# Seed exponents of a Fourier-domain SSM kernel: one product and four exponentials per chunk instead of 25 exponentials, with a new instruction order

## The chip, the cores and the metric

The kernel runs on one core of one Trainium2 chip. The metric is the device time of one execution in microseconds (us). Besides the times there is one profiled execution, whose instructions are recorded on the engines: PE (matrix multiplications, with PEld for its weight loads), DVE (VectorE), ACT (ScalarE), POOL (GpSimd), and SP, whose queue issues nearly all DMA transfers.

## The reference, cut to what matters

Two state-space layers A and B (L = 2048 positions, D = 512 channels, N = 128 states) see the same input u, and a gate mixes their results:

```python
dt = jnp.exp(log_dt)[:, None]
logdA = dt * (A_re + 1j * A_im)
P = jnp.exp(logdA[:, :, None] * l[None, None, :])      # l = 0 .. 2047
K = jnp.einsum("dn,dnl,dn->dl", Cc, P, dt * Bc).real
y = irfft(rfft(pad(u)) * rfft(pad(K)))[:L] + u * Dskip
...
out = g * a + (1 - g) * b          # g = sigmoid((u * gate_w).sum(-1))
```

The magnitude of the powers P is exp(al · l), with al = dt · A_re (one number for each state and channel). Powers of all l are products of a few seeds: l is split into digits, and exp(al · l) is the product of one factor per digit.

## The kernel before, in words

**Tiling.** The channels are cut into NCH = 8 chunks of 64 channels; with the two layers a chunk has CH = 128 columns. The 128 states lie on the partitions. A chunk is built in NG = 8 groups of G = 16 columns, so there are NT = 64 tables T = 0 .. 63.

**Seeds.** `seed(c, parts)` writes for a chunk the factors exp(al · l) into two tiles. `ml` (128 x 128 x 16) has in columns 0 to 7 the factors for l = 0 to 7, in columns 8 to 15 those for l = 0, 8, .. 56. `mh` (128 x 128 x 12) has in columns 0 to 7 those for 256 l, in columns 8 to 11 those for 64 l, l = 0 to 3. Each has two copies, used in turn by even and odd chunks. Before the change every column is one ACTIVATE of 128 elements (one number per channel column, so the writes are 16 or 12 floats apart), with the factor l in its scale; columns that are all ones are set once by `memset`. 25 such ACTIVATEs per chunk are recorded as five steps of five (line 523). The input is row 0 of the tile `par`, which for chunks 1 to 7 is loaded from DRAM (`prd`) by `load_par`; `par` has two buffers. `seed_angles` then makes the integer phases `sa` on POOL and multiplies columns 8 to 11 of `mh` by the amplitude rho, also on POOL.

**Tables.** For each T, `tables` makes phases `ang` on POOL (two additions or products, line 271), magnitudes `mr` from `ml` and `mh` (two products, line 271, mostly POOL), sine `s`, sine of the half `ang` and its square `sq` on ACT (three ACTIVATEs, line 284), and then on DVE `ei` = s · mr and `mr` = (sq − 1) · mr (lines 271 and 281, four instructions). `mr` has three buffers, `ang` and `ei` two, `s` and `sq` one each, in PSUM. In every third table the product of `ml` is made on DVE from a copy of eight columns in PSUM (`c`, copied by ACT). PE then multiplies these tables (`kgen`, line 588), a copy takes the result to `kt`, and `first` (line 605) begins the transform.

**The convolution.** Per chunk: `spectrum` (line 618) on PE, the product with the stored spectrum of u on DVE (`y`, line 690), the inverse `back` (line 710), copies to `z`, a store to DRAM `zb`, a transposed load to `f`, and `fin` (line 742) with a copy to `o` and the output's store. `u_spectra` and `gated` run once near the start. Copies out of PSUM (`copy`) may be made by ACT (line 294) or by DVE (line 296); `tt` with "any" by POOL or by DVE.

**What sets the order.** All work is first listed as steps, with their dependences. The string `ORDER` then gives the order in which the steps are issued; a number with `b` takes the second engine of the step's choice (DVE instead of ACT for a copy, DVE instead of POOL for an "any" product). Each engine works through its own steps strictly in this order, and SP issues its transfers in it. A buffer of a ring goes to the next user in this order.

**Tables of functions.** Exp and Sin lie in different function tables of ACT, so a change between them puts an ACT_TABLE_LOAD ahead of the instruction. Sine takes the table numbered 9 in the code, exponentials table 0.

Of the kernel before, what the change touches and what calls it, by code (L numbers as in the profile page):

```python
# [45 lines left out]
def constants():  # L46
# [7 lines left out]
    for q in range(4):  # L54
# [17 lines left out]
                                   np.full((128, 1), math.pi / 4)], 1).astype(f32)  # L72
# [10 lines left out]
6 7 11 8 9 4 2 182 3 1 82 83 0 84 475 86 186 183 18 19 20 24 21 22 23 25 26 27 28 29 30 31 32 33 34 35 37 88 184b 185b 38 17  # L83
36 85 190 326 40 44 45 39 41 42 46 47 48 366 76 49 50 51 59 79 73 71 75 187 52 53 188 189 54 55 56 57 138 58 191 193b 61 62
67 63 60 68 192 64 69 91 14 351 87 13 218 194 15 16 98 65 70 92 93 101 94 95 89 96 43 72 66 353 77 354 78 90 74 100 99 195
102 357 104 103 105 219 113 197b 196b 198 200 355 356 221b 114 360 358 359 199 201 385 203 205 386 361 107 204 206 106 220
226 127 222 327 202 207 210 213 208 209 211 212 129 80 97 12 368 369 383 367 81 10 384 362 108 363 109 110 111 215 214 370
364 216 365 223 112 116 115 371 224 373 122 121 117 123 374 225 372 388 124 118 119 120 387 375 227 217 1403 230 125 126 128
131 134 376 228 389 136 133 231 352 132 137 135 130 5 1406 229 429 232 377 233b 244 390 378 245 391 392 393 249 394 251 395
430 250b 397 398 399 400 401 246 402 403 479 247 477 476 480 478 141 396b 404 405 406 142 143 239 144 252b 145 146 248 1414  # L90
253 148 149 234 150 151 152 407 254 240 431 416 414 427 415 154 139 140b 153 235b 155 236 418 408 379 419 420 409 237 483 417
421 422 428 410 445 446 447 147 448 241 242 156 157 432 380 381 423 159 424 435 158 436 411 433 434 437 413b 438 382 412 160
458 459 481 255 262 175 238 258 484 449 450 257 256 425 439 161 163 452 451 426 440 485 460 482 441 461 162 259 165 166 260
261 453 172 171 173 174 454 263 462 463 265b 167 164 455 168 169 612 611 464 264 609 613 177 266 179 243 176 328 330 331 290
329b 465 267 269b 268b 466 456 457 610 487 467 468 280 282 281b 469 283b 488 470b 294 284 486 170 180 499 501 616 489 502 490
491 492 471 500 442 493 518 519 516 517 494 472 444 443 503 504 495 496 506 332 275 505 473 474 531 333 507 508 520 521 509
276b 497 510 498b 522 511 532 523 524 529 533 530 277 285 278 287 270 272 286 534 535 288 525 526 536 547 549 550 548 512 537
538 334 335 608 279 289 527 336 551 539 540 552 271 553 560 562 561 554 555 528b 541 337 273 564 542 513 563 556 339 178 338
557 558 579 514 515 567 568 580 565 559 566 581 577 543 578 582 593 591 592 594 1407 1408 569 570 585 1404 544 586 583 546
584 545 340 587 588 1405 595 596 341 571 572b 598 342 1415 1426 614 618 615 573 619 599 1416 597 1425 617 181 1417 1409 1410  # L100
1411 274 1412 589 633 590 622 623 349 345 1427 600 1418 1419 601 574 602 575 576 624 603 620 621 649 347 343 625 634 626 1420
# [100 lines left out]
def ssm_mix(ctx: ExitStack, tc: tile.TileContext, a, out, dry=False):  # L202
# [123 lines left out]
    def memset(name, o, *keys):  # L326
        op("pool", "memset", 128, lambda _: pool.memset(o(), 1.0), (), keys or [(name,)])
# [184 lines left out]
    def seed(c, parts):  # L512
# [3 lines left out]
        for k0, kn in parts:  # L516
            ks = slice(k0, k0 + kn)
            for n in range(0, len(cols), 5):
                some = cols[n:n + 5]

                def exps(_, ks=ks, some=some):
                    for tile, j, l in some:
                        act.activation(out=t(*tile)[:, ks, j], in_=t("par", c)[:, 0, ks].bitcast(F32), func=AF.Exp, scale=float(l))  # L523
# [311 lines left out]
```

## Time and profile before

| | |
|---|---|
| median of 3 runs | 477.8 us (475.12 to 482.99) |
| the profiled execution's own time | 472.5 us |
| its span, first to last instruction | 470.7 us |
| mean granted clock of TensorE | 0.971 |
| busy: PE / DVE / ACT / POOL | 394.9 / 416.0 / 386.2 / 338.8 us |
| ACT_TABLE_LOADs | 31, 1.283 us each |
| ACTIVATEs of `seed` | 200 |

The span is the recorded part; 1.8 us lie around it. Busy time is time in which at least one instruction of the engine runs. Of consecutive instructions on an engine the end of one overlaps the start of the next, so the mean duration times the count can exceed the busy time: a recorded ACTIVATE of `seed` lasts 423 ns, but five in a row take 1.3 us.

### The profile page before, as it was taken

How to read it: one execution, taken by the hardware profiler on the slowest of the kernel's cores; microseconds unless marked ns; L12 is line 12 of the kernel's file. 1: busy time of each engine (PE TensorE's matmuls, PEld its weight loads, DVE VectorE, ACT ScalarE, POOL GpSimd, SP SyncE). 2: the span in 40 equal slices, each digit the busy share in tenths (PEclk: the TensorE clock that was granted, in tenths of full speed). 3: DMA queues.
4: the chain of work that ended last, by engine and by line, in shares of the span. 5: the costliest groups of instructions: out<-in, count | busy, mean ns of one | idle time of the engine just before them, and what ended most of it. 6: DMA issues, size and time to landing. Idle time of an engine off the chain costs nothing.

```text
span 470.7 us, 21838 instructions
## 1 busy us (share of the span) xinstructions
PE 394.9 (84%) x9616; PEld 356.4 (76%) x9616; DVE 416.0 (88%) x518; ACT 386.2 (82%) x676; POOL 338.8 (72%) x317
## 2 busy tenths in 40 slices
PE   4797786799968879998898988879598888999935
PEld 3786685689857768787798977778587877898934
DVE  6999889999999999999899999998789999996610
ACT  3889979999988999998899999998789898791110
POOL 2593859599977989796999689878929899650010
PEclk9899899999998999999999999999999999999987
DMA  7866852836555565876465646764838667567793
GB/s 220 276 198 205 246 161 78 249 120 224 183 157 157 133 160 180 212 206 178 132 180 153 206 132 190 193 182 117 195 105 218 167 192 213 152 184 187 212 244 89
DMA packets 74542, 84.53 MB, mean 180 GB/s; under 512 B 5456, under 2 KB 60112, under 8 KB 73392
## 3 DMA queue, kind: packets, MB, share of 16 engines
q1 hardware_dynamic: 74304, 82.75, 62.0%
q8 instruction: 75, 1.23, 1.1%
q0 software_dynamic: 144, 0.39, 0.3%
q14 instruction: 19, 0.16, 0.1%
HBM read 51.48 MB, written 31.65 MB: 177 GB/s over the span
## 4 chain that ended last, share of the span: by engine, by line
PE 35%; DVE 25%; ACT 21%; issue 11%; DMA 4%; SPq 3%; DVEq 0%; POOL 0%; ACTq 0%
PE c L618 8%; PE c L605 8%; DVE mr L281 6%; PE c L588 6%; PE c L742 5%; PE c L710 4%; DVE y L690 4%; ACT s L284 4%; DVE ei L271 4%; ACT ang L284 3%; ACT sq L284 3%; SPq L289 3%; ACT ml L523 2%; DVE ei L281 2%; PE c L439 2%
## 5 line engine op out<-in xcount | busy, mean ns | idle before, releaser
L281 DVE SCALAR_TENSOR_TENSOR mr<-sq,mr 128x1024 f32<-128x1024 f32 (+1 forms) x128 | 117.4, 947 | 1.9 <-ACT sq L284 1.5
L271 POOL TENSOR_TENSOR mr<-ml 128x1024 f32<-128x1024 f32 x43 | 84.3, 1960 | 12.3 <-PE c L588 7.7
L271 POOL TENSOR_TENSOR ang<-par,cint 128x512 int32<-128x512 int32 x64 | 67.5, 1055 | 31.0 <-ACT sq L284 15.9
L271 DVE TENSOR_TENSOR ei<-s,mr 128x1024 f32<-128x1024 f32 x64 | 77.7, 1214 | 4.1 <-ACT s L284 2.8
L588 PE MATMUL c<-mr 128*32 128x64 f32 x2048 | 64.7, 223 | 14.8 <-DVE mr L281 7.3
L605 PE MATMUL c<-small,kt 128*64 128x128 f32 x1024 | 66.3, 283 | 10.9 <-issue 5.0
L690 DVE TENSOR_TENSOR y<-c,u 128x1024 f32<-128x1024 f32 x57 | 68.7, 1214 | 4.3 <-PE c L618 1.7
L284 ACT ACTIVATE s<-ang 128x1024 f32<-128x1024 int32 x64 | 65.9, 1029 | 6.5 <-POOL ang L271 4.5
L605 PEld LDWEIGHTS c<-small,kt 128*64 128x64 f32 x1024 | 58.2, 141 | 15.4 <-issue 6.3
L271 POOL TENSOR_TENSOR mr<-mh 128x512 f32<-128x512 f32 x63 | 67.7, 1080 | 2.4 <-PE c L588 2.4
L271 POOL TENSOR_TENSOR ang<-sa 128x512 int32<-128x512 int32 x64 | 68.6, 1073 | 0.2
L284 ACT ACTIVATE ang<-ang 128x1024 f32<-128x1024 int32 x64 | 67.7, 1058 | 1.2
L284 ACT ACTIVATE sq<-ang 128x1024 f32<-128x1024 f32 x64 | 66.0, 1032 | 3.2 <-DVE mr L281 2.3
L588 PEld LDWEIGHTS c<-mr 128*32 128x32 f32 x2048 | 48.6, 110 | 25.5 <-issue 9.9
L588 PE MATMUL c<-ei 128*32 128x64 f32 x2048 | 64.1, 221 | 3.2 <-issue 3.2
L710 PE MATMUL c<-y,vv 64*64 64x128 f32 x1792 | 59.9, 274 | 4.6 <-issue 2.7
L710 PEld LDWEIGHTS c<-y,vv 64*64 64x64 f32 x1792 | 50.9, 134 | 10.6 <-issue 5.2
L618 PE MATMUL c<-xa,w 128*128 128x128 f32 x384 | 52.8, 287 | 3.5 <-DVE vv L414 1.3
L618 PE MATMUL c<-xb,w 128*128 128x128 f32 x384 | 50.0, 282 | 4.7 <-DVE xb L296 1.3
L588 PEld LDWEIGHTS c<-ei 128*32 128x32 f32 x2048 | 50.6, 111 | 3.6 <-issue 3.6
L618 PEld LDWEIGHTS c<-xa,w 128*128 128x128 f32 x384 | 46.4, 194 | 7.7 <-issue 3.6
L618 PEld LDWEIGHTS c<-xb,w 128*128 128x128 f32 x384 | 45.1, 191 | 8.5 <-issue 3.1
(109 smaller groups left out, 661.9 us busy)
## 6 DMA issues: line engine op xcount, KB each, us to landing
zb<-z SPq DMA_DIRECT2D x31, 512.0 KB, 3.9
u<-us SPq DMA_DIRECT2D x57, 256.0 KB, 4.4
f<-zb SPq DMA_DIRECT2D x28, 512.0 KB, 5.2
us<-z SPq DMA_DIRECT2D x16, 512.0 KB, 3.7
uin<-in_uk_dram SPq DMA_DIRECT2D x16, 256.0 KB, 3.9
f<-in_ut_dram SPq DMA_DIRECT2D x8, 512.0 KB, 5.3
out_dram<-o SPq DMA_DIRECT2D x29, 128.0 KB, 3.2
par<-prd SPq DMA_DIRECT2D x7, 320.0 KB, 3.9
```

What stands on the lines that cost most here:

```text
L271: lambda e: (dve if e == "dve" else pool).tensor_tensor(out=out(), in0=in0(), in1=in1(), op=o),
L281: lambda _: dve.scalar_tensor_tensor(out=out(), in0=in0(), scalar=s, in1=in1(), op0=o0, op1=o1), reads, writes, port=port)
L284: op("act", "act", n, lambda _: act.activation(out=out(), in_=in_(), func=func, **{k: v() if callable(v) else v for k, v in kw.items()}), ...
L289: lambda e: (sp if e == "sp" else pool).dma_start(out=out(), in_=in_()), reads, writes, touch=touch)
L439: pe.matmul(t(*ps)[:, CH * i:CH * i + CH], V(x)()[:, CH * i:CH * i + CH], dgv()[:, k, i], start=True, stop=True)
L523: act.activation(out=t(*tile)[:, ks, j], in_=t("par", c)[:, 0, ks].bitcast(F32), func=AF.Exp, scale=float(l))
L588: pe.matmul(ps[32 * j:32 * j + 32, o], x[:, 4 * o + j, 64:96], x[:, 4 * o + j, 0:64], start=part == 0, stop=part == 1, tile_position=(0, 3 ...
L605: pe.matmul(t(*ps[g // 4])[64 * r:64 * r + 64, 128 * (g % 4):128 * (g % 4) + 128], t(*x)[:, g], t("small")[:, 128 * r:128 * r + 128], star ...
L618: pe.matmul(view()[:, :, k], t("w2", j // 2)[:, 4 * (j % 2) + k], t(*x1)[:, 4 * j + k], start=True, stop=True)
L690: op("dve", "tt1", 1024, lambda _: dve.tensor_tensor(out=t(*y).rearrange("p h s f d -> p h s (f d)"), in0=fv().rearrange("p s f d -> p s ( ...
L710: pe.matmul(bank_of(x)[64 * e:64 * e + 64, CH * q:CH * q + CH], v[:, 0:64] if h else v[:, 32:96], t(*ys[f // 4])[64 * x:64 * x + 64, h, :, ...
L742: pe.matmul(t(*ps)[64 * r:64 * r + 64, DC * i:DC * i + DC], t("gsi")[:, 4 * k + i, s, 64 * r:64 * r + 64], t(*f)[:, 8 * k + 2 * i + r, DC ...
```

## The change

`seed` now first writes, for the whole chunk, the eight products al · l for l = 0 to 7 into columns 0 to 7 of `ml` (one instruction of 1024 elements; the factors 0 to 7 lie in eight new columns of the constant `small`). Four ACTIVATEs follow, each with input from those columns: `mh` columns 0 to 7 with scale 256 (1024 elements), `mh` columns 8 to 11 with scale 64 (512), `ml` columns 8 to 15 with scale 8 (1024), and `ml` columns 0 to 7 in place (1024). The columns for l = 0 come out of the exponential too, so the six memsets of `ml` and `mh` are gone.

```diff
-        cols = [(mh, l, 256 * l) for l in range(1, 8)] + [(mh, 8 + l, 64 * l) for l in range(4)]
-        cols += [(ml, l, l) for l in range(1, 8)] + [(ml, 8 + l, 8 * l) for l in range(1, 8)]
+        runs = ((mh, 0, 8, 256.0), (mh, 8, 4, 64.0), (ml, 8, 8, 8.0), (ml, 0, 8, 1.0))
         for k0, kn in parts:
             ks = slice(k0, k0 + kn)
-            for n in range(0, len(cols), 5):
-                some = cols[n:n + 5]
-
-                def exps(_, ks=ks, some=some):
-                    for tile, j, l in some:
-                        act.activation(out=t(*tile)[:, ks, j], in_=t("par", c)[:, 0, ks].bitcast(F32), func=AF.Exp, scale=float(l))
...
+            tt("any", kn * 8, lambda ks=ks: t(*ml)[:, ks, 0:8],
+               lambda ks=ks, kn=kn: t("par", c)[:, 0, ks].bitcast(F32).unsqueeze(2).to_broadcast([128, kn, 8]),
+               lambda kn=kn: t("small")[:, 513:521].unsqueeze(1).to_broadcast([128, kn, 8]), OP.mult,
+               par(c, "al") + [("small",)], lq)
+            for tile, j, n, scale in runs:
+                actv(kn * n, lambda tile=tile, j=j, n=n, ks=ks: t(*tile)[:, ks, j:j + n], lambda n=n, ks=ks: t(*ml)[:, ks, 0:n],
+                     AF.Exp, lq, hq if tile == mh else lq, table=0, scale=scale)
...
-    for k in range(2):
-        for n, j in (("mh", 0), ("ml", 0), ("ml", 8)):
-            memset(n, lambda n=n, j=j, k=k: t(n, k)[:, :, j], *((n, k, q) for q in range(CH // QK)))
```

The string `ORDER` is replaced as a whole: every engine's queue stands in another order, and some steps take another engine. Counted over the built programs, per engine: the 200 ACTIVATEs of `seed` become 24 of 1024 elements and 8 of 512; the table loads go from 31 to 21; the eight new products stand on POOL. Of the copies, DVE's `kt` go from 17 to 13, `o` from 6 to 5, `xa` from 12 to 9, `xb` from 15 to 14, `z` from 28 to 19, and ACT's go up by as many (one `o`, four `kt`, four `xa` and `xb`, nine `z`). Of the products `mr` from `ml` in SBUF DVE takes 3 (before none, POOL 43, now 40), of those from `mh` 3 (before 1, POOL 63, now 61). One output store moves from POOL's queue to SP's. PE's work is the same, instruction for instruction, in another order.

ACT, where the seeds of chunk 1 are made (tables of chunk 0 around them; `par_724` and `par_699` are chunk 1's parameters, `ml_1`, `mh_1` its seeds; buffer numbers differ between the programs). Before:

```order
L284 ACTIVATE sq_847<-ang_833 128x1024
L523 ACT_TABLE_LOAD
L523 ACTIVATE ml_1_192<-par_724 128x128 x5
L294 ACTIVATE z_779<-c_841 128x512
L523 ACTIVATE mh_1_194<-par_724 128x128 x10
L523 ACTIVATE ml_1_192<-par_724 128x128 x5
```

Now:

```order
L284 ACTIVATE sq_818<-ang_764 128x1024
L294 ACTIVATE z_767<-c_809 128x512
L284 ACT_TABLE_LOAD
L284 ACTIVATE mh_1_194<-ml_1_192 128x128x8
L284 ACTIVATE mh_1_194<-ml_1_192 128x128x4
L294 ACTIVATE vv_0_199<-c_852 128x512
L284 ACTIVATE ml_1_192<-ml_1_192 128x128x8 x2
L284 ACT_TABLE_LOAD
```

What read `par` on ACT now reads `ml`, which POOL has written just before.

POOL, where the seeds of chunk 4 begin while the tables of chunk 3 start (`par_1053` is chunk 2, `par_1917` chunk 3, `par_2691` chunk 4; chunk 4 takes chunk 2's buffer of `par`). The new program:

```order
L271 TENSOR_TENSOR ang_2569<-par_1053,cint_201 128x16x32
L271 TENSOR_TENSOR ang_2569<-sa_1898 128x16x32
L271 TENSOR_TENSOR mr_2681<-mh_0_193 128x16x32
L271 TENSOR_TENSOR sa_2689<-par_1917,cint_201 128x1536
L271 TENSOR_TENSOR ml_0_191<-par_2691,small_183 128x128x8
L271 TENSOR_TENSOR mr_2694<-ml_1_192 128x16x64
```

Before, POOL had at the same place (`par_1102` is chunk 2, `par_1945` chunk 3) no instruction of chunk 4:

```order
L271 TENSOR_TENSOR ang_2782<-par_1102,cint_201 128x16x32
L271 TENSOR_TENSOR mr_2764<-mh_0_193 128x16x32
L271 TENSOR_TENSOR ang_2782<-sa_1931 128x16x32
L271 TENSOR_TENSOR sa_2786<-par_1945,cint_201 128x1536
L271 TENSOR_TENSOR ang_2788<-par_1945,cint_201 128x16x32
```

The product for chunk 4 stands four places behind the last reader of the buffer into which its input is loaded, and ahead of the first table product of chunk 3.

DVE, at the first tables of chunk 1 (`mr_1297` and `mr_1301` are their magnitudes). Now:

```order
L271 TENSOR_TENSOR mr_1297<-c_1291,ml_1_192 128x16x64
L296 COPY z_1299<-c_1281 128x512
L271 TENSOR_TENSOR mr_1301<-ml_1_192 128x16x64
L296 COPY kt_1295<-c_1303 128x256
L271 TENSOR_TENSOR mr_1297<-mh_1_194 128x16x32
L271 TENSOR_TENSOR ei_1350<-s_1341,mr_1297 128x16x64
```

Before, with the same table of chunk 1 (`mr_1404`):

```order
L296 COPY z_1368<-c_1358 128x512
L296 COPY z_1368<-c_1363 128x512
L271 TENSOR_TENSOR mr_1404<-c_1354,ml_1_192 128x16x64
L296 COPY kt_1347<-c_1370 128x256
L271 TENSOR_TENSOR ei_1445<-s_1420,mr_1404 128x16x64
```

Two products of `ml` and `mh`, which POOL made before, are DVE's here, and one copy of `z` is no longer DVE's.

More of the change, by code (lines that the diff above doesn't have):

```diff
@@ L87 @@
[L87 to L94, printed above, removed]
```

105 lines of the change are left out of this document (51 added, 54 removed), and 32 rows, old and new, of the table ORDER.

## The prediction

> **What bounds the kernel now.** I read the profile from the whole to the part: the page's busy times, a table of stretches, the chain of work that ended last, and the groups by shape.
>
> ```profile
> span 470.7 us, 21838 instructions
> PE 394.9 (84%) x9616; PEld 356.4 (76%) x9616; DVE 416.0 (88%) x518; ACT 386.2 (82%) x676; POOL 338.8 (72%) x317
> core 0: us, PE busy (x) PEld busy (x) DVE busy (x) ACT busy (x) POOL busy (x), PEclk, DMA share, GB/s
> 0.00:20.00 20.00, 10.85 (x115) 9.83 (x116) 15.32 (x46) 12.01 (x29) 5.91 (x14) 0.96 0.83 254
> 20.00:60.00 40.00, 32.98 (x497) 30.62 (x497) 34.50 (x49) 35.08 (x77) 28.78 (x30) 0.93 0.68 211
> 60.00:320.00 260.00, 227.76 (x5636) 204.36 (x5637) 254.01 (x299) 242.60 (x413) 219.87 (x197) 0.99 0.60 170
> 320.00:360.00 40.00, 32.71 (x924) 29.24 (x922) 32.99 (x38) 34.62 (x65) 29.30 (x26) 0.96 0.65 163
> 360.00:425.00 65.00, 58.69 (x1716) 52.57 (x1708) 62.38 (x71) 55.21 (x83) 52.99 (x49) 1.00 0.65 182
> 425.00:471.00 46.00, 31.91 (x752) 29.82 (x752) 16.77 (x19) 6.65 (x14) 2.00 (x4) 0.89 0.70 184
> ```
>
> The 88% of DVE is an average over three parts that differ. From 60 to 320 us DVE is busy for 254.0 of 260 us, 98%; ACT has 242.6 (93%), PE 88%, POOL 85%. In the last 46 us DVE has little to do. The last table's magnitudes end on DVE at 424.9:
>
> ```profile
> 423.05 1.81 DVE L281 SCALAR_TENSOR_TENSOR mr<-sq,mr 128x1024 f32<-128x1024 f32 x2
> ```
>
> What follows (the last products y, the last inverse, store, load, `fin`) is 46 us in which the change does nothing: the same instructions stand behind the last table on PE, and DVE has one copy of `xb` less there. So the time is the moment of the last table plus 46 us, and what counts is how fast DVE gets through the tables. Nevertheless the chain of work that ended last runs often over ACT, as this part of it shows (140 to 200 us, shares of 60 us):
>
> ```profile
> by line: ACT s L284 10.0%; issue 9.8%; ACT ml L523 9.7%; ACT ang L284 8.9%; ACT sq L284 7.8%; PE c L588 7.4%; ACT L523 6.4%; ACT L284 6.4%; DVE y L690 5.8%; DVE mr L281 5.6%; ACT xa L294 4.2%; ACT mh L523 4.1%; PE c L710 3.3%; DVE mr L271 2
> ```
>
> The seeds (ml and mh, L523) are 13.8% of these 60 us, and the table loads (the nameless ACT L523 and L284) 12.8%. But in the same stretches DVE idles for almost nothing: a chain over ACT is not free time on DVE. These two readings are the two forecasts between which I choose.
>
> **ACT, step by step.**
>
> ```profile
> L523 ACT ACTIVATE ml<-par 128x128 f32<-128x128 f32 x112 | 29.5, 423 | 0.1
> L523 ACT ACTIVATE mh<-par 128x128 f32<-128x128 f32 x88 | 24.4, 435 | 0.1
> L523 ACT ACT_TABLE_LOAD x13 | 16.7, 1283 | 0.2
> L284 ACT ACT_TABLE_LOAD x18 | 23.1, 1283 | 1.0 <-PEq L824 0.7
> L284 ACT ACTIVATE ang<-ang 128x1024 f32<-128x1024 int32 x64 | 67.7, 1058 | 1.2
> L294 ACT ACTIVATE z<-c 128x512 f32<-128x512 f32 x63 | 36.0, 596 | 12.0 <-PE c L710 9.3 <-PE c L618 2.7
> L284 ACT ACTIVATE c<-ml 128x128 f32<-128x128 f32 x21 | 5.9, 281 | 0.1
> L294 ACT ACTIVATE kt<-c 128x256 f32<-128x256 f32 x47 | 18.0, 382 | 5.5 <-PE c L588 5.5
> ```
>
> Removed: 29.5 + 24.4 = 53.9 us of seeds, and ten table loads of 1.283, 12.8 us. Added: 24 exponentials of 1024 elements. No row has their form, with runs of eight floats 16 apart in and out. Nearest is `ang`, 1.058 us, in place in SBUF; and `c` from `ml` reads just such runs at 281 ns for 128 elements, no more than a dense copy's slope gives (382 at 256, 596 at 512). The far end is the old form's rate, 53.9/200 = 0.27 us for 128 elements, 2.16 for 1024; the near end is 1.03 (`sq`). I take 1.058, since `c` shows that runs of eight cost nothing to read. With 8 of 512 at 0.6 this makes 25.4 + 4.8 = 30.2 us. Copies taken over from DVE: nine `z` and four `xa`, `xb` at 0.596, four `kt` and one `o` at 0.38, 9.6 us. ACT changes by −53.9 − 12.8 + 30.2 + 9.6 = **−26.9 us**; at the far end of the price it would be +3.5.
>
> **DVE.**
>
> ```profile
> L296 DVE COPY z<-c 128x512 f32<-128x512 f32 x25 | 16.3, 679 | 0.3 <-PE c L710 0.3
> L296 DVE COPY kt<-c 128x256 f32<-128x256 f32 x17 | 7.0, 414 | 2.4 <-PE c L588 2.4
> L271 DVE TENSOR_TENSOR mr<-c,ml 128x1024 f32<-128x1024 f32 x21 | 25.5, 1214 | 1.5 <-ACT c L284 1.5
> L271 DVE TENSOR_TENSOR mr<-mh 128x512 f32<-128x512 f32 x1 | 0.8, 769 | 0.0
> ```
>
> Thirteen copies of 512 go (0.68 each), four `kt` and an `o` (0.41): −10.9 us. Two `mr` from `mh` come (0.77 each). Three `mr` from `ml` with both inputs in SBUF come; this form has no row, between 1.21 (one input in PSUM) and POOL's 1.96. I take 1.3, as the `mh` form shows 0.77 against 0.68 for other work of its size: +3.9. Together **−5.5 us** (−3.5 at the far end).
>
> **POOL.**
>
> ```profile
> L271 POOL TENSOR_TENSOR mr<-ml 128x1024 f32<-128x1024 f32 x43 | 84.3, 1960 | 12.3 <-PE c L588 7.7 <-ACT ml L523 1.7 <-issue 1.1
> L271 POOL TENSOR_TENSOR mr<-mh 128x512 f32<-128x512 f32 x63 | 67.7, 1080 | 2.4 <-PE c L588 2.4
> POOL ang L271 <- ACT sq L284: 15.9, 11, 4.3
> ```
>
> Eight products of 1024 elements at 1.96 are +15.7; three and two tables' products leave, −5.9 and −2.2; the memsets and an output's issue are −2.4. POOL gains 5.2 us. It is hidden: POOL is 85% busy in the middle, and it waits 15.9 us because ACT has not yet freed `ang`; it runs ahead. Without that lead the whole product would come into the path of every chunk (rival three).
>
> **What of it reaches the end.** DVE's 5.5 us lie in the part where it is saturated, so I count them in full. ACT's 26.9 us count only where DVE waited for ACT:
>
> ```profile
> DVE ei L271 <- ACT s L284: 2.8, 4, 1.8
> DVE mr L281 <- ACT sq L284: 1.5, 5, 0.6
> DVE mr L271 <- ACT c L284: 1.5, 2, 1.0
> ```
>
> That is 5.8 us. In a new order some such waits arise elsewhere; I take half, −2.9, with 0 and −5.8 as ends. The start is costed at nothing: four exponentials take the place of two groups of five before the first sine, some 0.6 us earlier, but the chain there lies on PE and DMA. Three more things are left as they are. The wait of 4 us inside a run of PE's multiplications, put down to issue, which idles DVE for 5.1,
>
> ```profile
> 339.79 3.16 PE L605 MATMUL c<-small,kt 128*64 128x128 f32 x28 [4.02 <-issue]
> DVE xb L296 <- PE c L605: 5.1, 1, 5.1
> ```
>
> has no cause in the order that I can see; gone, it is worth up to −5. PE keeps all its instructions and the part behind the last table. The output store that leaves POOL lies in the tail, where POOL waits.
>
> **The sum:** 470.7 − 5.5 − 2.9 = 462.3 us of span, with the 1.8 around it 464.1, against this execution's own 472.5. The median of the runs shown, 477.8, is 1.011 times that execution, so the forecast is 464.1 · 1.011 = **469 us**, 1.8% less. About 2% (below 468.2 or above 487.4) is what a measurement of this kernel can tell from no change, as its runs lie between 475 and 483; the forecast is just inside.
>
> **Rivals.**
>
> *One: the chain over ACT pays in full.* Another part of the chain, 260 to 320 us, looks like the one above:
>
> ```profile
> by line: issue 16.3%; DVE mr L281 11.9%; ACT s L284 8.1%; PE c L605 8.0%; DVE ei L271 6.0%; ACT ang L284 5.3%; DVE y L690 5.3%; ACT sq L284 4.5%; ACT mh L523 4.5%; ACT L284 4.3%; ACT z L294 4.1%; ACT ml L523 4.0%; PE c L742 3.5%; ACT L523 2
> ```
>
> In both parts together seeds are 8.3 + 5.1 us and table loads 7.7 + 3.8. Seeds fall to 30.2/53.9 = 0.56 of their time, loads to 21/31: −5.9 and −3.7. With DVE's 5.5 the gain is 15.1, 457.4 in this execution's terms, 462.5 by the median. For it: seeds stand on the chain. Against it: DVE would then have to fill 98% of the middle without its remaining small waits.
>
> *Two: nothing is gained.* POOL, ACT and DVE all stand above 85% in the middle; if the new order's waits take back 8 us, or the runs of eight cost ACT their far price, it is 478.
>
> *Three, the other side: the seeds come late, through POOL.* The product heads POOL's queue until `par` has landed, and ACT's exponentials behind it wait in turn, with the whole product in between.
>
> ```profile
> par<-prd SPq DMA_DIRECT2D x7, 320.0 KB, 3.9
> 225.78 1.08 POOL L271 TENSOR_TENSOR ang<-sa 128x512 int32<-128x512 int32 x1
> 226.93 2.83 POOL L271 TENSOR_TENSOR sa<-par,cint 128x1536 int32<-128x1536 int32 x1
> ```
>
> For chunk 4 the product stands behind only 1.08 + 1.08 + 2.83 = 5.0 us of POOL's work after its buffer is free; the load takes 3.9 once it is issued, and SP's queue may be waiting for a store then. Queued behind the product is the next table's `mr`. Lost per chunk would be 3.9 + 1.96, less the 2.9 by which four exponentials are shorter than 25 (6.7 against 3.8): 3.0, for seven chunks 21. Less DVE's 5.5 that is +15.5 for this execution, 493 by the median; half of it gives 485. It decides once POOL has no lead left, three `mr` buffers or some 18 us of tables (400 us of middle over 64 tables, 6.2 each). The 15.9 us of POOL's waits for ACT speak against it.
>
> *Four: DVE's products with two SBUF inputs are held up by POOL.* There are six instead of one. The one row is mild: 769 ns, while a POOL product ended beside it in its usual 1.95 us and the next `sa` took 3.27 instead of 2.83.
>
> ```profile
> 374.97 0.77 DVE L271 TENSOR_TENSOR mr<-mh 128x512 f32<-128x512 f32 x1
> 373.24 1.95 POOL L271 TENSOR_TENSOR mr<-ml 128x1024 f32<-128x1024 f32 x1
> 375.15 3.27 POOL L271 TENSOR_TENSOR sa<-par,cint 128x1536 int32<-128x1536 int32 x1
> ```
>
> If each of the six waited for a whole POOL product of 1.96, DVE would lose 12 us, 481 by the median; by this row it loses 0.5. The Trainium skill ("SBUF — State Buffer", Who interferes with whom) says that a DVE instruction with both inputs in SBUF contends with a GpSimd instruction that reads SBUF, and that whoever is second is blocked for the whole instruction. By that rule this rival would hold; the row shows 0.09 us on DVE and 0.44 on POOL, not 1.95, so the trace agrees that they meet, not with the size.
>
> **How the numbers follow.** Forecast 0.50, with its own range 463 to 475, of which 0.21 lies below 468.2; rival one 0.20; two 0.12; three 0.10; four 0.08. Faster by over 2%: 0.21 + 0.20 = 0.41. Slower by over 2%: half of rival three to all of it, with the edges of four: 0.10. Within: 0.49. The range for 8 in 10 leaves out rival three and the lower part of rival one: 456 to 482, which takes in −5.8 instead of −2.9, the issue wait, and rival four.
>
> **What the changed profile would show.** Right: 24 exponentials of 1024 at about 1.06 us and 8 at 0.6; ACT near 359 us busy, DVE near 410.5, POOL near 344; DVE still about 98% from 60 to 320; the last `mr` some 8 us earlier and 46 us to the end. Exponentials at 2 us would take ACT's gain away. POOL waiting for `par`, or ACT's first exponential waiting for POOL by over 2 us at several chunks, is rival three; `mr` from `ml` on DVE at over 2 us is rival four. The last `mr` 15 us earlier is rival one. I am also wrong if the new order moves DVE's waits for PE, which I held constant.

## The result, and the profile after

| | before | changed |
|---|---|---|
| median of 6 runs each | 476.5 us (470.5 to 483.0) | 479.8 us (477.0 to 482.0) |
| ratio | | 1.0119, 95% interval 1.0071 to 1.0167 |
| the profiled execution, its span | 472.5, 470.7 us | 477.4, 475.6 us |
| mean granted clock of TensorE | 0.971 | 0.964 |
| last table's `mr` ends on DVE | 424.9 us | 430.2 us |

The forecast was 1.8% less; it became 1.2% more by the ratio (0.7% by the medians). The change is slower, by less than 2%. A ratio with an interval leaves out disturbed runs; where too few runs were left for one, medians of all runs are compared.

The page of the changed kernel, its stretches and the end of its last table, in the columns of those of before:

```profile
span 475.6 us, 21661 instructions
PE 400.1 (84%) x9616; PEld 359.9 (76%) x9616; DVE 416.0 (87%) x505; ACT 362.7 (76%) x516; POOL 349.9 (74%) x313
20.00:60.00 40.00, 32.53 (x506) 29.58 (x506) 38.28 (x56) 33.20 (x48) 28.04 (x26) 1.00 0.71 225
60.00:320.00 260.00, 227.92 (x5564) 204.45 (x5563) 247.04 (x285) 223.21 (x308) 224.85 (x196) 0.97 0.60 168
428.38 1.82 DVE L281 SCALAR_TENSOR_TENSOR mr<-sq,mr 128x1024 f32<-128x1024 f32 x2
```

ACT lost 23.5 us of work and DVE none. DVE's share from 60 to 320 us nevertheless fell from 98 to 95%: it has 3.8 us more to do between 20 and 60 us, 7.0 less between 60 and 320, and it idles more there. Up to the end of the last table it is busy for 399.6 us (before 399.1) and idle for 30.6 (25.8). The loss, 5.3 us, lies ahead of that moment; the tail is 45.4 us (45.8). It does not grow evenly: by the ends of DVE's last `mr` of each table, the changed kernel is 0.5 us ahead of before at table 26, 9.4 behind at table 35, 2.5 ahead at table 48 and 5.3 behind at the last.

The new pieces by shape (ACT, POOL, then DVE):

```profile
L284 ACT ACTIVATE ml<-ml 128x1024 f32<-128x1024 f32 x16 | 16.8, 1052 | 0.2
L284 ACT ACTIVATE mh<-ml 128x512 f32<-128x512 f32 x8 | 5.0, 623 | 0.0
L271 POOL TENSOR_TENSOR ml<-par,small 128x1024 f32<-128x1024 f32 x8 | 16.7, 2088 | 4.5 <-DMA par<-prd 2.9 <-DVE mr L271 1.6
L296 DVE COPY z<-c 128x512 f32<-128x512 f32 x17 | 11.5, 683 | 2.0 <-PE c L710 1.2 <-PE c L618 0.8
L271 DVE TENSOR_TENSOR mr<-ml 128x1024 f32<-128x1024 f32 x3 | 4.3, 1437 | 0.0
L271 DVE TENSOR_TENSOR mr<-mh 128x512 f32<-128x512 f32 x3 | 2.8, 918 | 0.0
```

The prices of the exponentials (1.052 and 0.623 us against 1.058 and 0.6) and of POOL's product (2.09 against 1.96) were about right. What DVE waited for, changed kernel, 60 to 425 us:

```profile
DVE mr L281 <- ACT sq L284: 5.8, 7, 3.1
DVE ei L271 <- POOL mr L271: 3.9, 5, 2.1
DVE kt L296 <- PE c L588: 3.1, 2, 1.7
DVE ei L271 <- PE c L588: 2.6, 1, 2.6
DVE ei L271 <- issue: 2.0, 1, 2.0
```

Before, POOL did not appear among these releasers at all, and ACT's `sq` stood at 1.5. In all DVE waits 22.0 us between 60 and 425 (before 15.6). In a second profile of the changed kernel the sum is much the same, 23.5, but not its parts: there DVE waits 4.7 us for ACT, as before (4.8), 4.0 for POOL and 10.5 for PE (before 9.6), and 4.3 stand under issue. POOL's part has come in both profiles; ACT's has grown only in the first.

### The profile page after: what moved, and what is told of

Its sections match the earlier page's. It is cut to its first block, busy times and chain, and to the rows that moved or that the text cites. A ratio compares the mean times of both kernels' runs of the same rounds, so it can differ in the third digit from the quotient of the medians.

```text
span 475.6 us, 21661 instructions
## 1 busy us (share of the span) xinstructions
PE 400.1 (84%) x9616; PEld 359.9 (76%) x9616; DVE 416.0 (87%) x505; ACT 362.7 (76%) x516; POOL 349.9 (74%) x313
## 4 chain that ended last, share of the span: by engine, by line
PE 33%; DVE 29%; issue 13%; ACT 11%; POOL 7%; DMA 4%; SPq 1%; DVEq 0%; ACTq 0%; POOLq 0%
PE c L618 8%; PE c L605 7%; PE c L588 6%; DVE mr L281 6%; PE c L710 5%; DVE ei L271 4%; DVE y L690 4%; PE c L742 3%; POOL mr L271 3%; ACT s L284 3%; ACT sq L284 2%; POOL ang L271 2%; DVE mr L271 2%; ACT ang L284 2%; POOL sa L271 2%
## 5 line engine op out<-in xcount | busy, mean ns | idle before, releaser
L271 POOL TENSOR_TENSOR mr<-ml 128x1024 f32<-128x1024 f32 x40 | 78.6, 1967 | 9.7 <-PE c L588 8.6
L271 POOL TENSOR_TENSOR ang<-par,cint 128x512 int32<-128x512 int32 x64 | 68.9, 1077 | 21.8 <-ACT sq L284 21.2
L588 PE MATMUL c<-mr 128*32 128x64 f32 x2048 | 67.1, 226 | 18.3 <-DVE mr L281 6.8
L271 POOL TENSOR_TENSOR mr<-mh 128x512 f32<-128x512 f32 x61 | 65.9, 1085 | 7.4 <-PE c L588 5.2
L588 PE MATMUL c<-ei 128*32 128x64 f32 x2048 | 65.7, 223 | 3.9 <-issue 3.9
L588 PEld LDWEIGHTS c<-mr 128*32 128x32 f32 x2048 | 49.8, 112 | 25.0 <-issue 15.3
L710 PEld LDWEIGHTS c<-y,vv 64*64 64x64 f32 x1792 | 52.0, 136 | 12.5 <-issue 6.0
L618 PE MATMUL c<-xa,w 128*128 128x128 f32 x384 | 54.4, 290 | 3.4 <-ACT xb L294 1.6
L618 PE MATMUL c<-xb,w 128*128 128x128 f32 x384 | 52.4, 286 | 3.1 <-DVE mr L271 1.0
L294 ACT ACTIVATE z<-c 128x512 f32<-128x512 f32 x71 | 40.2, 592 | 17.0 <-PE c L710 11.5
```

The lines of the kernel that those rows point to most:

```text
L271: lambda e: (dve if e == "dve" else pool).tensor_tensor(out=out(), in0=in0(), in1=in1(), op=o),
L294: act.activation(out=o(), in_=i(), func=AF.Copy)
L588: pe.matmul(ps[32 * j:32 * j + 32, o], x[:, 4 * o + j, 64:96], x[:, 4 * o + j, 0:64], start=part == 0, stop=part == 1, tile_position=(0, 3 ...
L618: pe.matmul(view()[:, :, k], t("w2", j // 2)[:, 4 * (j % 2) + k], t(*x1)[:, 4 * j + k], start=True, stop=True)
L710: pe.matmul(bank_of(x)[64 * e:64 * e + 64, CH * q:CH * q + CH], v[:, 0:64] if h else v[:, 32:96], t(*ys[f // 4])[64 * x:64 * x + 64, h, :, ...
```

## The experiments

Kernels of one set ran side by side and shared the runs of the kernel before. Orders are lists of step numbers; a `b` takes a step's second engine. Programs with the old seeds and with the new number their steps differently. Medians of the kernel before differ between the sets, from 474.4 to 477.9 us, so a comparison across sets is worth less than one within a set.

### Set one: each half of the change alone

**New seeds in the old order.** Old steps keep their places and engines; the product stands some 20 steps ahead of the first exponential. Chunk 1:

```diff
-... 401 246 402 403 479 247 477 476 480 478 141 ...
+... 384 372 470 239 385 386 387 243 ... 397 241 471 472 473 474 135 ...
```

> The new seeds (one product on POOL, four exponentials) in the instruction order of the kernel before, with every copy and product on the engine it had there; only the seeds' own steps differ, the product standing some 20 steps ahead of the first exponential. Theory 1 (the seeds gain, the new order loses): ACT loses about 53.9 - 30.2 us of seeds and some table loads, DVE's small waits for ACT shrink, DVE's busy time stays at 416; 3 to 6 us faster than before, ratio 0.987 to 0.995. Theory 2 (the seeds themselves cost, by POOL's eight products of about 2 us or by what they hold up on DVE): 2 to 6 us slower, ratio 1.005 to 1.012, with DVE's SBUF-to-SBUF work longer than before. Theory 3 (neither counts, since ACT is not what DVE waits for): 0.995 to 1.005.

485.1 us median (481.6 to 492.8) against 477.9 of before (467.1 to 485.1), by the medians 1.015, above all three ranges. Its trace (of its longest run) shows where much of it goes: the product of chunk 1 stood ahead of its load, and the next table's sine behind it.

```profile
54.32 2.06 POOL L271 TENSOR_TENSOR ml<-par,small 128x1024 f32<-128x1024 f32 x1 [8.39 <-DMA par<-prd]
58.45 1.03 ACT L284 ACTIVATE s<-ang 128x1024 f32<-128x1024 int32 x1 [9.44 <-POOL ang L271]
```

The fourth table ends 6.4 us later than before. This is the mechanism of rival three of the prediction, which had 3.0 us a chunk, brought about by where I put the product; in the changed kernel POOL's products wait 2.9 us for `par` in all.

**Old seeds in the new order.**

```diff
-... 470 409 471 410 ... 411 425 421 422 135 ... 472 134 473 474 402 ...
+... 476 477 416 379 417 ... 427 428 141 ... 478 140 479 480 408b ...
```

> The 25 exponentials per chunk in the instruction order of the changed kernel, at the places of its four exponentials; the product is left out of POOL, the memsets are back. ACT has some 24 us more work than the changed kernel, the table loads stay near 21. Theory 1 (seeds gain, order loses): slower than the changed kernel by the 3 to 6 us that the seeds bring, ratio to before 1.018 to 1.025. Theory 2 (the seeds cost): at or below before, 0.997 to 1.005. Theory 3 (neither): as the changed kernel, 1.007 to 1.017.

490.4 us (486.6 to 494.8), 1.026 by the medians, just above theory 1's range. Slower than the changed kernel by 11 us, within this set: in the new order ACT has no room for 18 us more (381.1 busy against 362.7; 24 were expected). So ACT's work does count in the new order.

**The six products back on POOL.**

```diff
-349b 483b 495b 707b 1075b 1189b
+349 483 495 707 1075 1189
```

> The changed kernel with the three products of ml and the three of mh that stand on DVE put back on POOL, at the same places of the order. DVE loses 3 x 1.437 + 3 x 0.918, about 7 us of busy time, POOL gains about 9. Theory P (what the copies freed on DVE was given back by these products and by what POOL's traffic does to DVE's products of two SBUF inputs): if DVE is the limit, up to 7 us faster, ratio to before 0.997 to 1.004. Rival (these products stand where POOL is the late engine, and DVE has idle time there): no gain or a loss, ratio 1.010 to 1.020, with DVE waiting for POOL instead.

491.9 us (488.0 to 493.9), 1.029 by the medians. DVE is busy for 5.1 us less, and the time is 12 us longer. Its waits, 60 to 425 us:

```profile
DVE mr L281 <- ACT sq L284: 9.6, 5, 8.2
DVE ei L271 <- POOL mr L271: 7.9, 6, 4.9
```

So theory P falls: at the places of these products POOL has no lead, and the new order needs them on DVE.

**The changed kernel again.**

> The changed kernel once more, as a control for the runs beside it and for a second profile. Ratio to before 1.007 to 1.017 again. If the pauses in the middle of PE's runs of multiplications that the profile puts down to issue belong to the program, they stand at the same instructions with the same lengths; if they are chance, their lengths differ and with them the moments at which DVE idles.

479.6 us (476.8 to 484.1); before's median was higher in this set, so 1.0035 by the medians. Five pauses that stand under issue, of 0.9 us or more, come back at the same multiplications of PE in this profile; three others above 0.7 us are in one of the two profiles alone. The longest was 3.57 us in the first profiled execution and 4.40 in this one, both here (PE's row of each):

```profile
219.47 0.22 PE L588 MATMUL c<-mr 128*32 128x64 f32 x1 [3.57 <-issue]
```

```profile
219.65 0.26 PE L588 MATMUL c<-mr 128*32 128x64 f32 x1 [4.40 <-issue]
```

### Set two: the price of the product and the worth of ACT's relief

**Products in gaps.** In the old order, chunk 1's product right ahead of its exponentials, the others where POOL had waited:

```diff
-... 470 239 385 386 387 243 ... 397 241 471 472 473 474 ...
+... 240 396 397 470 241 471 472 473 474 ...
```

> The new seeds in the order of the kernel before, as in the first of these runs, but with each chunk's product moved to a place where POOL waited in the profile of before (for chunk 1 right ahead of the exponentials, so that POOL doesn't stand behind the load of par; there it waited 8.4 us in the first run and the tables fell back by 6.2). Theory G (where the product stands in POOL's queue decides, not the exponentials): the 6.2 us of chunk 1 and some of the later losses come back, 3 to 8 us faster than the first run, ratio to before 0.995 to 1.003. Theory S (shorter seeds then pay as well): 0.987 to 0.995. Rival (POOL's 16 us of extra work cost wherever they stand): 1.007 or more.

476.4 us, ratio 0.9952 (0.9883 to 1.0020): theory G, though the interval reaches into S. 16 us of product in gaps cost nothing, and ACT's 30 us (386.2 to 355.7 busy) bring nothing, that can be told from zero. The seeds are those of the changed kernel, whose ratio is 1.0119 (1.0071 to 1.0167): the two intervals lie apart, so the loss comes with the new order and its engines, about 8 us.

**No product, old order.**

```diff
-            tt("any", kn * 8, lambda ks=ks: t(*ml)[:, ks, 0:8], ...)
...
+                     lambda n=n, ks=ks, kn=kn: t("par", c)[:, 0, ks].bitcast(F32).unsqueeze(2).to_broadcast([128, kn, n]),
```

> As the run beside it, but the product is left out and the four exponentials read par's first row with each number repeated, so all columns of a tile get the same factor: the seeds' values are not those of the reference, the number and the length of ACT's instructions are. This is ACT's relief alone, with nothing added on POOL. Theory S (ACT's 24 us and ten table loads lie on the path): 0.980 to 0.992. Rival (DVE doesn't wait for ACT, so a shorter ACT brings next to nothing): 0.994 to 1.002. The difference to the run beside it is the price of the products in gaps: nothing by theory G, 5 to 10 us by its rival.

474.9 us (467.1 to 479.4) against 476.1 by the medians, 0.3% less. Shorter seeds, for themselves, are worth next to nothing.

**No product, new order** (the same edit in the changed kernel).

> The changed kernel, its order and its engines, without the product (left out as in the run beside it). It prices the product where the changed kernel has it. If the product is hidden, as the prediction had it, the time stays within 1 us of the changed kernel, ratio to before 1.005 to 1.015; if it is on the path, up to 8 x 2 us come back, 0.975 to 1.000. The six products of ml and mh on DVE stay, so what they cost is not in it.

Ratio 1.0080 (1.0039 to 1.0120) against the changed kernel's 1.0119 (1.0071 to 1.0167): the product is worth 0.4% at most by these centres, and the intervals overlap. Without any product the new order is still slower than before.

**15 copies to ACT, old order.**

```diff
-259b 275b 492b 641b 1459b 733b 1773b 1526b 890b 311b 318b 1537b 1040b 1155b 1812b
+259 275 492 641 1459 733 1773 1526 890 311 318 1537 1040 1155 1812
```

> The first run of this call (new seeds, old order, products in gaps), and 15 of DVE's copies between the first tables and the last, every fourth, given to ACT at the same places of the order: ten of 512 elements at 0.68 us and five of 256 at 0.41, 8.9 us of DVE's work; ACT, freed of 24 us by the seeds, gains some 8. Theory D (DVE is the bound, and each us taken off it is a us of the end): 6 to 9 us faster than that first run. Rival (DVE's neighbours in the loop are as late as DVE itself, so its free time turns into waits): within 3 us of it, with DVE's idle time up by as much as its busy time is down.

Ratio 1.0037 (0.9978 to 1.0097); DVE's busy time fell by 6.2 us against products in gaps. At table 39 it was 3.6 us ahead of products in gaps (the kernel before was 3.1 ahead of it there, without any copy moved), then this came, on ACT:

```profile
308.55 0.60 ACT L294 ACTIVATE xb<-c 128x512 f32<-128x512 f32 x1 [5.12 <-PE c L605]
```

Behind the waiting copy stood a table load, three exponentials of a chunk and then a table's `sq`, for which DVE waited:

```profile
313.92 1.22 DVE L281 SCALAR_TENSOR_TENSOR mr<-sq,mr 128x1024 f32<-128x1024 f32 x1 [5.54 <-ACT sq L284]
```

### Set three: what a microsecond of each engine is worth

**Half of one product on DVE left out.**

```diff
-        stt(G * 64, lambda: t(*M)[:, :, 32:96], lambda: t(*Q), 1.0, ...)
+        w = 64 if T < 6 else 32
+        stt(G * 64, lambda: t(*M)[:, :, 32:32 + w], lambda: t(*Q)[:, :, 0:w], 1.0, ...)
```

> The kernel before, and from the seventh table on the product mr = (sq - 1) mr of 1024 elements on DVE (1.215 us each) takes only the first half of its columns; the rest of mr keeps the magnitudes, so the result is not the reference's. About 0.53 us less on DVE in 58 tables, 31 us, order and engines unchanged. It asks directly what the prediction took for granted, that DVE's work in the middle counts in full: then 27 to 31 us are gone at the end, ratio 0.935 to 0.945. Rival (the engines of the loop wait for each other and DVE is only one of several that are late): half of it or less, 0.965 to 0.995, with DVE's idle time up by 15 us or more.

Ratio 0.9895 (0.9832 to 0.9958): about 5 us for 25 us of DVE (416.0 to 390.7 busy; 31 were expected). By this the bound that the prediction read from 98% falls.

**Half of PE's kgen left out.**

```diff
-                for x, part in ((R, 0), (I, 1)):
+                for x, part in ((R, 0), (I, 1)) if T < 6 else ((R, 0),):
```

> The kernel before, and from the seventh table on PE multiplies only the real half of a table (64 of the 128 multiplications of kgen; the half with ei is left out, so the result is not the reference's). Some 1.0 us less on PE in 58 tables, about 58 us, the other engines' work unchanged. If DVE is the bound in the middle, PE's work is hidden there: only DVE's few waits for PE go, 0 to 8 us, ratio 0.983 to 1.0. If PE with its pauses is what the loop waits for, 20 us or more go, ratio below 0.96.

Ratio 0.9754 (0.9695 to 0.9814): 12 us for 21 us of PE's busy time (394.9 to 374.1; the cut was expected to take 58). By the microsecond, the engine that is busy for 88% pays more than twice as much as the one at 98%, though the gain is less than the 20 us that its theory asked for. PE no longer waits for `ei` in this run either, so not all of the gain need be PE's own time.

**Adding to DVE in the changed kernel.** 15 copies back from ACT, evenly spread:

```diff
-255 282 553 1416 1459 730 804 311 951 998 1114 1100 1636 1300 1304
+255b 282b 553b 1416b 1459b 730b 804b 311b 951b 998b 1114b 1100b 1636b 1300b 1304b
```

> The changed kernel with 15 of ACT's copies between the first tables and the last, evenly spread (ten of 512 elements, five of 256), given to DVE at the same places of the order: DVE gains 15 works of 0.68 and 0.41, 8.9 us, ACT loses about 7.9. It is the mirror of the run that took 15 copies off DVE in the old order. Theory C (copies on ACT wait for PE and hold up the sines behind them, which is what the new order loses by): 2 to 6 us faster than the changed kernel, ratio to before 0.998 to 1.007. Theory D (DVE is the bound): 7 to 9 us slower, 1.025 to 1.031. Theory O (an order fits its own set of engines, any change of it costs): 1.015 to 1.025.

Ratio 1.0202 (1.0150 to 1.0255), for 7 us more on DVE (423.0 busy). The changed kernel did not run in this set; against its run in the first, this is 4 us more by the ratios (1.0119) and 8 by the medians (488.0 and 479.8). That is theory O's range, its interval touches D's, and it is against C.

**The eight products on DVE** (each product's step gets a `b`).

> The changed kernel with the eight products of the seeds on DVE instead of POOL, at the same places: POOL loses 16.7 us, DVE gains 8 products with both inputs in SBUF, 1.2 to 1.8 us each, some 12 us. Leaving the product out altogether took 2 us off the changed kernel. Theory D (DVE is the bound): 8 to 12 us slower than the changed kernel, ratio to before 1.03 or more. Rival (POOL is as late as DVE where these products stand): within 3 us of it, 1.006 to 1.018.

Ratio 1.0352 (1.0300 to 1.0404), above the changed kernel by 11 us by the ratios and 15 by the medians, for 11 us more on DVE (426.7 busy). Work added to DVE in the changed kernel is paid, by half at the least in one run and in full in the other, though work taken away is not repaid.

### Set four: both reliefs, the other order, and chosen copies

**Less DVE and less ACT, old order** (the cut of DVE in the kernel without product).

> The old order with both reliefs: the new exponentials without their product (as in the earlier run, the factors are not the reference's), and from the seventh table on half of the 1024 elements of DVE's mr = (sq - 1) mr left out. DVE has 25 us less, ACT 30 us less than in the kernel before. Each alone brought 1% and 0.3% by the medians. Theory T (two engines in a ring with one buffer each: whichever is relieved, the other holds the pace): together 15 us or more, ratio to before 0.95 to 0.97. Rival (PE and POOL hold the pace): the sum of the two, 0.98 to 0.99.

Ratio 0.9757 (0.9695 to 0.9820), about 12 us, which would be more than the 6 of the two alone and less than theory T asked for. But this ratio rests on two of four runs (462.2 and 463.7 us; the others are 473.8 and 478.4), and by the medians (468.8 against 474.4) the gain is 6 us, the sum of the two alone. Whether DVE and ACT hold each other stays open.

**The cut of DVE in the changed kernel.**

> The changed kernel with the same half of mr = (sq - 1) mr left out from the seventh table on (25 us of DVE; the result is not the reference's). In the old order this brought 1%. Theory T (ACT held it there, and here ACT has 24 us less to do): 10 us or more below the changed kernel, ratio to before 0.97 to 0.99. Rival (POOL, which has the product here, or PE takes over): 3 to 6 us below it, 0.995 to 1.005.

Ratio 1.0107 (1.0059 to 1.0154), against 1.0119 uncut: 26 us off DVE (389.6 busy) bring nothing that can be told from zero, 479.7 us against 479.8. Theory T falls here, and so does its rival's 3 to 6 us.

**The cut of PE in the changed kernel.**

> The changed kernel with the half of kgen that multiplies ei left out from the seventh table on (about 20 us of PE's busy time as measured in the old order; the result is not the reference's). In the old order it brought 2.5%, 12 us. Theory P (the new order loses by waits behind PE): more than there, 15 us or more below the changed kernel, and the two orders come out alike, ratio to before 0.97 to 0.98. Rival (the loss is in waits for ACT and POOL, which a faster PE doesn't touch): 12 us or less, 0.985 to 0.995.

Ratio 0.9825 (0.9774 to 0.9876), 2.9% below the changed kernel's, 14 us: a little more than in the old order, between the two expectations.

**19 copies to ACT, chosen so that none waits for PE** (in products in gaps).

```diff
-407b 259b 323b 263b 804b 291b 311b 1569b 1570b 1132b 1416b 938b 522b 566b 890b 1168b 1186b 1812b 1155b
+407 259 323 263 804 291 311 1569 1570 1132 1416 938 522 566 890 1168 1186 1812 1155
```

> The new seeds in the old order, products in gaps, and 19 of DVE's copies on ACT, chosen by the profile of that kernel: in each case PE had ended what is copied before ACT came to this place, and most stand ahead of an exponential or another copy, not of a sine. Twelve of 512 elements at 0.68 us and seven of 256 at 0.41, 11.0 us off DVE. Of the 15 copies that were moved without this choice four had waited for PE, 1.0 to 5.1 us, with sines and exponentials behind them, and the gain of 3.6 us at table 39 was lost there. Theory W (it was those waits): 3 to 9 us faster than the kernel before, ratio 0.980 to 0.994. Rival (DVE's relief is worth nothing in any place): 0.995 to 1.004.

Ratio 0.9997 (0.9951 to 1.0042). Theory W falls. Against products in gaps DVE has 6.2 us less to do up to table 57 and idles 8.2 more. None of the versions that do the whole work beats the kernel before measurably; the best is products in gaps, 0.9952 with an interval that holds 1.

**Where DVE's relief goes.** I sum PE's waits from 60 to 425 us by releaser, from the rows of its waits in each trace:

```
                          DVE    issue   ACT    POOL   all
before                    20.4   14.3    7.7    2.2    44.6
old, products in gaps     21.6   12.6    7.0    2.2    44.0
old, 19 copies to ACT     16.1   11.9   15.3    2.6    46.1
old, cut of DVE           12.7   18.0   10.6    4.1    45.8
changed                   10.8   13.3   14.5    7.4    46.0
changed, second profile    9.8   15.3   12.0    9.4    47.2
new order, no product     11.1   16.3   13.4    9.0    49.8
changed, cut of DVE        6.2   21.9   12.7    9.3    50.1
```

The last column holds DMA's small rest as well. It stays at 44 to 50 us whatever is taken off DVE. The largest rows of before and of the changed kernel:

```profile
PE c L588 <- DVE mr L281: 6.4, 9, 1.9
PE c L605 <- issue: 5.4, 2, 4.0
PE c L605 <- POOL kt L271: 2.2, 3, 1.1
```

```profile
PE c L605 <- POOL kt L271: 6.9, 7, 2.3
PE c L588 <- issue: 6.6, 6, 3.6
PE c L588 <- DVE mr L281: 5.6, 5, 3.9
```

PE waits 10 us less for DVE in the changed kernel, and 7 more for ACT and 5 more for POOL (11 less, 4 and 7 more in the second profile). The 19 copies show the first exchange by itself: with nothing else changed, PE's wait for DVE falls by 5.5 and that for ACT rises by 8.3. The wait for POOL (mostly `kt`, the small addition behind a copy) is there without the product too, so it belongs to the order.

### Set five: PE's pauses

16 and 32 extra narrow multiplications early in PE's program, each of them recorded as two:

```diff
+            for _ in range(16 if name == ("u", 0, 1) else 0):
+                pe.matmul(t(*ps[0])[0:64, 0:16], t(*x)[:, 0], t("small")[:, 0:16], start=True, stop=True, tile_position=(0, 0))
```

> The changed kernel with 16 extra narrow multiplications (64 x 16, overwritten at once) ahead of PE's second group of u, where it waits for a load a moment later; 32 more recorded multiplications, about 1 us at the start. All later instructions of PE lie 32 records further on in its stream. Theory B (the pauses belong to blocks of the stream): each pause stands about 32 multiplications of the program earlier, the one of 3.6 to 4.4 us at the 3775th multiplication comes at another instruction with another length, and the sum changes; time within 5 us of the changed kernel on either side. Rival (the pauses belong to the moment, what the DMA queues do at 220 us, or to the instruction): the same pause at the same place, ratio 1.007 to 1.017.

> As the run beside it with 32 extra multiplications, 64 records, half a block. Theory B: pauses 64 multiplications of the program earlier, other lengths. If the pauses make the difference of the two orders, the three kernels that differ only in these extra multiplications (changed, 16, 32) differ in time by what their pauses differ, 3 us or more between the best and the worst, and one of them may reach the kernel before, ratio 0.998 to 1.020. If they lie beside other waits, all three stay at 1.007 to 1.017.

Ratios 1.0044 (0.9996 to 1.0093) and 1.0111 (1.0034 to 1.0187). Pauses over 0.7 us, by the number of the recorded multiplication (some of them):

```
changed again   248  360  976  2252   3775 (4.40)               4284  7977
shift 16        280  392 1008  2284          3903 (2.92)  4539        7978
shift 32        312  424 1040  2316          3903 (3.08)  4539        7978
```

There are two kinds. Those on the left move with the program and keep their lengths to 0.2 us (at the 360th 1.84 in all three): they belong to an instruction. Those on the right stand at fixed numbers of the stream, multiples of 127 or 128 apart, with other lengths: theory B. The queue of instruction packets fits that: before it has 75 packets of 16 KB for 9616 multiplications and as many weight loads, one for 256 of them, and 61 where half of kgen is left out.

```profile
q8 instruction: 75, 1.23, 1.1%
```

```profile
q8 instruction: 61, 1.00, 0.9%
```

The times of these packets, which the traces hold too, show what PE waits for (us):

```
               PE stops   packet of q8        PE goes on
before 6700     335.77    337.07 to 338.43     339.79
changed 3775    215.89    216.79 to 218.16     219.47
shift 16 3903   220.99    221.44 to 222.64     223.91
```

Over all twenty traces, 156 of the 161 pauses above 0.7 us that stand under issue end 1.2 to 1.8 us after such a packet has ended; of all multiplications, about one in ten begins at such a distance. So in these pauses PE waits for its next instructions. Why a packet comes late stays open.

Whether these pauses make the difference of the orders stays open too. Counted as gaps above 0.3 us inside a run, between 50 and 430 us, they are 18.0 and 21.2 us in the changed kernel's two executions against 14.8 to 17.3 in five of the old order's, which speaks for it. But the three other traces of the old order with all of PE's work (the first run of set one, and the two cuts of DVE) have 21.8 to 22.8, and the old seeds in the new order, at 490 us, have 15.1. Shift 16, the fastest of the three by its centre, has 22.0 us of them and shift 32 has 19.5, and all three intervals overlap. That speaks against it.

## Why the prediction went wrong, step by step

**The bound: wrong, and the root of it.** "What counts is how fast DVE gets through the tables" was read from DVE's 98%. Taking 25 us off DVE brought 5 us in the old order and nothing in the new one. DVE, ACT, POOL and PE hand each table on through one to three buffers; what DVE is relieved of turns into its own idle time and into PE's waits for the others. That a chain over ACT "is not free time on DVE" was right, but neither is DVE's time free time of the end.

**DVE −5.5 us, "counted in full": the step that failed,** in size and in weight. The copies went nearly as forecast, but DVE's busy time is the same: the six products took 7.1 us where the forecast's prices make 6.2, and operations that run once, between SBUF and SBUF, grew by some 3 us because other instructions of POOL now lie beside them (`ei` of 1536 elements from 1751 to 2852 ns: it starts 0.83 us into the new product of chunk 0 and waits out its rest; the eight `gsi` of line 667 from 867 to 1025). A true −5.5 would not have counted in full either: the cut of 26 us in the changed kernel brought nothing.

**ACT −26.9 us, of which −2.9 counts:** measured −23.5. In the old order nothing of it counts (0.3% without the product). DVE's waits for ACT, 4.8 us between 60 and 425, are 7.2 and 4.7 in the changed kernel's two profiles, instead of halving. In the new order the shorter seeds are needed, as 18 us of ACT put back cost 11, but the new order loses more than they save. The price of the exponentials was right.

**POOL +5.2 us, hidden:** measured +11.1 (338.8 to 349.9 busy), of which the product's longer time makes 1.0 and POOL's `ang`, 12 and 22 ns longer each, 2.2. The product itself is nearly hidden (0.4% by the centres in the new order, nothing in gaps of the old). But "POOL runs ahead" was wrong for the new order: six products had to go to DVE for it, and putting them back costs 12 us.

**Waits for PE and pauses held constant:** the prediction named this as what would make it wrong. DVE's row for PE's `xb` (5.1 us) went, as did the pause of 4.0 us behind it; pauses of PE of 3.6, 1.8 and 2.2 us came at other places, and DVE's waits for PE and issue sum to 10.0 us between 60 and 425, before 9.8. Held constant was right for this sum, by chance: in the second profile it is 14.8. The pause of 4.0 us for which the prediction saw no cause is one of those that end behind an instruction packet.

**The rivals.** One (the chain over ACT pays in full) is refuted by the old order without product. Two (nothing gained, the new order's waits take back 8 us, 478) is what happened, with 0.12 for it; it deserved most of the weight. Three is real at a badly chosen place (8.4 us) and small in the changed kernel (2.9). Four is the mechanism of DVE's lost 5.5 us, at less than half its price and mostly in places that I had not looked at.

**What is shown and what is not.** Shown: with the same seeds the new order and its engines lose about 8 us against the old one with the products in gaps; ACT's relief is worth nothing measurable in the old order, and DVE's nothing in the new; in the new order PE waits less for DVE and more for ACT and for POOL, in both profiles. Not shown to the last microsecond: which part of the 1.2% is those waits, which the product, and which PE's pauses; each is of the size of what the intervals leave open.

## What to carry to other kernels

A share of 98% does not say what a microsecond of that engine is worth; leaving out a piece of its work does: here 25 us were worth 5 in one order and nothing in the other. In a ring of engines with one to three buffers, read the waits of every engine by releaser, and expect relief of one to come back as waits for its neighbours; a change that lightens one engine and re-orders the others is forecast at no change until a cut shows otherwise. A copy that moves to an in-order queue carries its wait along: what stands behind it there pays.

## What the runs showed of the hardware that I had not expected

**DVE waits for the rest of POOL's instruction.** A `TENSOR_SCALAR` of 512 elements in SBUF takes 0.42 us alone; 0.29 us behind the start of POOL's product of 2.08 us it took 2.07, and ended 0.28 us after that product. Changed kernel, DVE and POOL:

```profile
81.59 0.42 DVE L420 TENSOR_SCALAR gsi<-vv 128x512 f32<-128x512 f32 x1
83.25 2.07 DVE L420 TENSOR_SCALAR gsi<-vv 128x512 f32<-128x512 f32 x1
82.96 2.08 POOL L271 TENSOR_TENSOR ml<-par,small 128x1024 f32<-128x1024 f32 x1
```

The other way round too: in the changed kernel's second profile DVE's `mr` from `ml` took 1.85 us (1.21 at 96.9 us, without POOL), and POOL's next `ang`, behind it, 2.05 instead of 1.06.

```profile
96.90 1.21 DVE L271 TENSOR_TENSOR mr<-ml 128x1024 f32<-128x1024 f32 x1
358.72 1.85 DVE L271 TENSOR_TENSOR mr<-ml 128x1024 f32<-128x1024 f32 x1
358.44 1.05 POOL L271 TENSOR_TENSOR ang<-par,cint 128x512 int32<-128x512 int32 x1
359.44 2.05 POOL L271 TENSOR_TENSOR ang<-sa 128x512 int32<-128x512 int32 x1
```

So the rule of the Trainium skill ("SBUF — State Buffer", Who interferes with whom) that the second of the two is blocked until the first has ended holds here to 0.3 us. The prediction set it aside by a row in which DVE had come when only 0.2 us of POOL's product were left (374.97 against 373.24 + 1.95): the row agreed with the rule, and I had read it without its start times.

**PE stops at block borders of its instruction stream,** one in 127 or 128 recorded multiplications, for anything up to 5.7 us (the cut of DVE without product), the long stops at the same numbers in both profiles of the changed kernel. It goes on 1.2 to 1.8 us after a 16 KB packet of the instruction queue has ended; what makes the packet late was not tried.
